# A gated attention and MLP kernel: smaller and reordered first loads, and a new order of the products that build the first K projection

## Chip, cores and metric

The kernel runs on one core of one Trainium2 chip. The metric is the device time of one execution in microseconds; a kernel is told by the median of several runs.

## What is computed

The reference takes `x` (2048 rows of 512), and gives `g * a + (1 - g) * b` in float32:

```python
g = _sigmoid((x * gate_w).sum(-1, keepdims=True))
qkv = x @ wqkv                       # 32 heads of 16
pq, pk = per-head q @ w_phi, k @ w_phi
phi = concat(softmax(p), softmax(-p))      # for q and for k
kv, z = phi_k^T v, sum over rows of phi_k
o = (phi_q kv) / (phi_q z + 1e-6)
a = o @ wo
b = mish(x @ w1 + b1) @ w2                 # 512 -> 1376 -> 512
```

The per-head 16 x 16 matrices `w_phi` come right behind the projections, so the kernel folds them into the weights first: `wk_fused = wk @ blockdiag(w_phi)`, and the same for `wq`. This folding is called "fusing" below.

## The kernel before, in words

**Precision.** The large products use `float32r` operands, one TensorE pass each. Every operand is split into a high part (a copy rounded to `float32r`) and a low part (the rest), and a product is the sum of three: high x high, high x low and low x high. The small fusing products and the warming products use plain float32; each of those shows as two MATMUL records in the profile.

**Stages.** Stage A goes through `x` in 8 chunks of 256 rows (`NCH`), two half-chunks `t` of 128 rows each: K, V and Q projections (`proj`, 12 products of 128x512 each, four blocks `k` of the contraction times three parts), feature maps, and a running sum of phi_k^T v (`kvp`). Stage B goes through 4 blocks of 512 rows: the MLP (`up`, `down`), attention (`num`) and the output product (`wo`). Texts such as `FIRST` and `EVEN` (lines 39 to 86) are the order of the steps, written out by hand, and `keep_in_program_order` (`pin`) keeps each engine's instructions in the order of the code.

**The opening**, which the change touches, stands ahead of the text `FIRST`:

- Loads (lines 139 to 166). SyncE (SP) issues, in this order: block 0 of the transposed K weights (`skT`, tensor `wkT`, 256 KB a block), blocks 0 and 1 of the first chunk of `x` (`rawx[0]`, 256 KB), K block 1, `x` blocks 2 and 3, K blocks 2 and 3, two pieces of the V weights (512 KB each), four blocks of the Q weights (`wqT`), the next chunk of `x`. ScalarE's own queue issues one load at the start: the block diagonal `bd` of `w_phi` into `bds` (256 KB, 2 KB a partition).
- Warming (lines 169 to 177). `warm(n)` multiplies a tile of ones by itself `n` times into a scratch bank and nothing reads it. `WARM` (line 34) is 10; two more stand behind the first fuse (line 706).
- Fusing K (lines 218 to 224 and 700 to 711). `fuse(acc, skT, k)` makes 16 float32 products of 64x64 out of K block `k` and `bds` into two PSUM banks; there are four such banks (tag `dn`), so two blocks are under way at a time. `fsplit(acc, k)` then makes the high part `wkh` of the block with two ScalarE copies, and the low part `wkl` with two VectorE subtractions.
- Splitting `x`. `x_hi(0, j)` is a ScalarE copy of `x` blocks `2j` and `2j+1` (128x512), and `x_lo(0, j, V)` a VectorE subtraction of the same shape.
- The first K projection. `k_part(k)` (line 692) makes the six products of block `k`: parts high x high, low(x) x high, high x low(w), each for the two half-chunks, into the two banks `pk`.

The loop of lines 700 to 714 says the order: fuse 0, two warming products, fuse 1; then x split 0, fsplit 0, x split 1, fsplit 1; then `k_part(0)`, `k_part(1)`; then fuse 2, fuse 3, fsplit 2 and fsplit 3. The split of the V weights follows on ScalarE, VectorE and GpSimd (lines 715 to 718), and then `k_part(2)` and `k_part(3)`. `FIRST` goes on with `fq` (the four fuses of the Q weights, line 724), and `v0`, the first V projection.

A helper records most operations under one line: all products have L101, ScalarE copies L121. They are told apart by the names of their tiles.

Of the kernel before, what the change touches and what calls it, by code (L numbers as in the profile page):

```python
# [15 lines left out]
P = 128  # L16
# [4 lines left out]
KT = D // P  # L21
NG = 4
SC = 256
# [7 lines left out]
NF = NFA + NFB  # L31
GROW = FA % P
ORDER = [NFA - 1] + list(range(NFA - 1)) + list(range(NFA, NF))
WARM = 10

# [52 lines left out]
def tile_gated_mix(ctx: ExitStack, tc: tile.TileContext, xT, wv, wkT, wqT, bd, w1a, w1b, b1, w2a, w2b, wo, out):  # L90
# [6 lines left out]
    pin = tc.keep_in_program_order  # L97
    V, G_, A_, Sy = nc.vector, nc.gpsimd, nc.scalar, nc.sync

    def mm(*a, **k):  # L100
        return pin(nc.tensor.matmul(*a, **k))  # L101
# [5 lines left out]
    def k8(name, tag, dt=F32R):  # L107
        return T([P, 2048], dt, tag, 2 if tag in ("eT", "E") else 1, name)

    def k4(name, tag, dt=F32):  # L110
        return T([P, 1024], dt, tag, {"tx": 2, "oh": 2, "z": 1}[tag], name)

    def k2(name, tag, dt=F32):
        return T([P, 512], dt, tag, {"pq": 3, "io": 4, "hl": 8}[tag], name)

    def psum(name, tag, bufs={"a": 3, "dn": 4, "kv": 1}):
        nm[0] += 1
        return pp.tile([P, 512], F32, name=f"{name}_{nm[0]}", tag=tag, bufs=bufs[tag])

    def act(out_, in_, fn=AF.Copy, **k):  # L120
        return pin(A_.activation(out_, in_, fn, **k))  # L121

    def kt(t, f):
        return t[:, : KT * f].rearrange("p (k f) -> p k f", f=f)
# [4 lines left out]
    def f32(ap):  # L129
        return ap.bitcast(F32)  # L130
# [5 lines left out]
    def stage(wT):  # L136
        return T([P, NFA * 512], F32, "w1a", 2, "wT")[:, : KT * 512].rearrange("p (k g f) -> p k g f", k=KT, f=P)

    skT, sqT = stage(wkT), stage(wqT)
    bds = k2("bds", "io")[:, :].rearrange("p (g f) -> p g f", g=NG)  # L140
    pin(A_.dma_start(bds, bd))
    rawx = {}

    def ldx(c):
# [3 lines left out]
    def ldk(dst, src, k):  # L148
        pin(Sy.dma_start(dst[:, k, :, :], src[:, k, :, :]))

    ldk(skT, wkT, 0)
    rawx[0] = k4("xraw", "tx")
    for j in range(2):
        pin(Sy.dma_start(kt(rawx[0], SC)[:, 2 * j : 2 * j + 2, :], xT[0][:, 2 * j : 2 * j + 2, :]))
        ldk(skT, wkT, j + 1)
    ldk(skT, wkT, 3)

    def piece(dram, o, n=1024):
        r = k4("raw", "oh")
# [13 lines left out]
    def warm(n):  # L173
        for _ in range(n):
            mm(pw[:, :P], ones, ones, start=True, stop=True)

    warm(WARM)
    onr = const.tile([P, P], F32R, name="onr")
# [25 lines left out]
    def run(text, key, prev=None, nxt=None):  # L204
# [6 lines left out]
    wkh, wkl, wvh, wvl, wqh, wql = [  # L211
        kt(k8(n, t), 512) for n, t in (("wkh", "xbh"), ("wkl", "xbl"), ("wvh", "woh"), ("wvl", "wol"), ("wqh", "eT"), ("wql", "eT"))]
    xs, Es, vs, psA, Ep = {}, {}, {}, {}, {}
# [4 lines left out]
    def fuse(acc, staged, k):  # L218

        for G in range(NG):  # L220
            o = (k % 2 * NG + G) * 64
            for r in (0, 64):
                for c in (0, 64):
                    mm(acc[r // 64][c : c + 64, o : o + 64], staged[r : r + 64, k, G, c : c + 64], bds[r : r + 64, G, r : r + 64], start=True, stop=True, skip_group_check=True)

    def fuse_banks():
        return [psum("fuse", "dn") for _ in range(2)]

    def halves(w, ks):
        return [w[:, ks, :].rearrange("p k (g r f) -> p r (k g) f", r=2, f=64)[:, r, :, :] for r in range(2)]  # L230
# [15 lines left out]
    def x_hi(c, j):  # L246
        act(xs[c][0][j], kt(rawx[c], SC)[:, 2 * j : 2 * j + 2, :])

    def x_lo(c, j, eng):
        pin(eng.tensor_sub(xs[c][1][j], kt(rawx[c], SC)[:, 2 * j : 2 * j + 2, :], f32(xs[c][0][j])))  # L250
# [430 lines left out]
    def fsplit(acc, k):  # L681
        wh, wl = halves(wkh, slice(k, k + 1)), halves(wkl, slice(k, k + 1))
        src = [a[:, k % 2 * 256 : k % 2 * 256 + 256].rearrange("p (g f) -> p g f", f=64) for a in acc]
        for r in range(2):
            act(wh[r], src[r])
        for r in range(2):
            pin(V.tensor_sub(wl[r], src[r], f32(wh[r])))

    new_x(0)
    pk = {}  # L690

    def k_part(k):
        for n, (a, w) in enumerate(((xs[0][0], wkh), (xs[0][1], wkh), (xs[0][0], wkl))):
            for t in range(2):
                sl = slice(t * P, (t + 1) * P)
                if t not in pk:
                    pk[t] = psum("proj", "a")
                mm(pk[t], a[k // 2][:, k % 2, sl], w[:, k, :], start=(k == 0 and n == 0), stop=(k == KT - 1 and n == 2))

    for ks in ((0, 1), (2, 3)):  # L700
        acc = []
        for k in ks:
            acc.append(fuse_banks())
            fuse(acc[-1], skT, k)
            if k == 0:
                warm(2)
        for k in ks:
            if k < 2:
                x_hi(0, k)
                x_lo(0, k, V)  # L710
            fsplit(acc[k % 2], k)
        if ks[0] == 0:
            k_part(0)
            k_part(1)
    for j in range(2):
        h, l = [w[:, 2 * j : 2 * j + 2, :].rearrange("p k f -> p (k f)") for w in (wvh, wvl)]
        act(h, wvr[j])
        pin((V, G_)[j].tensor_sub(l, wvr[j], f32(h)))
    k_part(2)
    k_part(3)  # L720

    accq = []

# [86 lines left out]
```

## Time and profile before

| what | value |
|---|---|
| median of 3 runs | 450.23 us (449.79, 450.23, 450.31) |
| the profiled execution | 449.95 us |
| its span, first to last instruction | 448.2 us |
| TensorE busy (PE) | 443.4 us, 99% of the span |
| VectorE, ScalarE, GpSimd busy | 307.0, 195.1, 164.7 us |
| chain that ended last | PE 98%, DMA 1% |
| Start of the first fuse, of the first K product | 5.95 us, 7.84 us |
| Start of the first fuse of the Q weights | 15.24 us |

Times inside the profile are microseconds from the start of the span. PE is a matrix product, PEld its weight load, DVE is VectorE, ACT ScalarE, POOL GpSimd, and SPq and ACTq are the issue of DMAs on SyncE's and ScalarE's queue. A row of the timeline gives start, duration, engine, line, operation, output <- inputs, shape, and how often it stands in a row; in brackets the idle time of the engine ahead of it and what ended that. Durations of neighbouring products overlap, so what a product costs is read from the distance of starts.

### The profile page before, as it was taken

The page shows a single profiled execution, that of the slowest core. Times are in us where ns is not written, and L with a number is a line of the kernel's source. Part 1 is how long each engine was busy: PE and PEld are TensorE (multiplying, and loading weights), DVE is VectorE, ACT ScalarE, POOL GpSimd, SP SyncE. Part 2 cuts the span into 40 slices and gives each one's busy share as a digit, 9 for nine tenths or more (in the row PEclk, how much of TensorE's full clock was granted, in tenths as well). Part 3 has the DMA queues.
Part 4 walks back from the last instruction along what each step waited for, and adds up shares of the span by engine and source line. Part 5 has one row for each costly group of instructions (what it writes and reads, how often), then busy time and mean ns, then how long its engine had stood idle before and what let it go on. Part 6 is the DMA issues. An engine that isn't in the chain of part 4 may idle for free.

```text
span 448.2 us, 7221 instructions
## 1 busy us (share of the span) xinstructions
PE 443.4 (99%) x2886; PEld 363.7 (81%) x2886; DVE 307.0 (68%) x408; ACT 195.1 (44%) x269; POOL 164.7 (37%) x102
## 2 busy tenths in 40 slices
PE   8999999999999999999999999999999999999997
PEld 7888888888888888878788878888878888887885
DVE  2798559459398999997989998369769329701103
ACT  3644533444335465627255352644262653242330
POOL 3448687677861445521122220214220222221121
PEclk9999999999999999999999999999999999999999
DMA  7721623615523100405243151321241302030002
GB/s 278 264 95 47 190 66 99 191 14 173 189 75 115 48 24 20 123 15 142 81 108 127 38 153 53 89 95 47 54 134 48 94 1 95 17 78 1 1 0 95
DMA packets 25882, 40.09 MB, mean 89 GB/s; under 512 B 5748, under 2 KB 14196, under 8 KB 25848
## 3 DMA queue, kind: packets, MB, share of 16 engines
q1 hardware_dynamic: 25528, 39.22, 29.2%
q8 instruction: 23, 0.38, 0.3%
q10 hardware_dynamic: 288, 0.39, 0.3%
q14 instruction: 11, 0.09, 0.1%
q0 software_dynamic: 32, 0.01, 0.0%
HBM read 22.82 MB, written 8.40 MB: 70 GB/s over the span
## 4 chain that ended last, share of the span: by engine, by line
PE 98%; DMA 1%; ACT 0%; DVE 0%; issue 0%
PE proj L101 30%; PE up L101 27%; PE down L101 27%; PE wo L101 10%; PE kvp L101 2%; PE num L101 2%; DMA bds<-in_bd_dram 1%; PE fuse L101 1%; PE rest L101 0%; PE z L101 0%; ACT wkh L121 0%; PE warm L101 0%; DVE io L653 0%; PE kvT L459 0%
## 5 line engine op out<-in xcount | busy, mean ns | idle before, releaser
L503 POOL TENSOR_TENSOR l<-act,h 128x512 fp32r<-128x512 f32 x44 | 63.8, 1452 | 218.1 <-ACT h L121 183.8
L121 ACT ACTIVATE act<-up,b1s 128x512 f32<-128x512 f32 x44 | 30.3, 689 | 92.1 <-PE up L101 91.2
L323 POOL TENSOR_TENSOR zacc<-zacc,E 128x1024 f32<-128x1024 f32 x16 | 39.8, 2485 | 43.9 <-DVE E L285 42.6
L121 ACT ACTIVATE E<-E 128x1024 f32<-128x1024 f32 x32 | 33.4, 1058 | 37.7 <-DVE E L270 37.6
L285 DVE TENSOR_TENSOR E<-E,Sm 128x1024 f32<-128x1024 f32 x32 | 46.6, 1456 | 1.1
L274 DVE TENSOR_REDUCE Sm<-E 128x64 f32<-128x1024 f32 x32 | 38.5, 1204 | 5.0 <-ACT E L121 5.0
L101 PE MATMUL wo<-woh,ohl 128*128 128x512 f32 x128 | 41.2, 389 | 0.0
L101 PE MATMUL down<-w2ah,h 128*128 128x512 f32 x96 | 37.7, 393 | 0.0
L101 PE MATMUL down<-w2al,h 128*128 128x512 f32 x96 | 37.4, 390 | 0.0
L101 PE MATMUL down<-w2ah,l 128*128 128x512 f32 x96 | 37.4, 389 | 0.0
L258 DVE TENSOR_REDUCE mx<-proj 128x32 f32<-128x512 f32 x16 | 11.0, 689 | 32.0 <-PE proj L101 32.0
L101 PE MATMUL down<-w2bh,h 128*128 128x512 f32 x78 | 30.6, 392 | 0.0
L101 PE MATMUL down<-w2bl,h 128*128 128x512 f32 x78 | 30.4, 390 | 0.0
L101 PE MATMUL down<-w2bh,l 128*128 128x512 f32 x78 | 30.3, 389 | 0.0
L408 DVE TENSOR_TENSOR xbl<-xraw,xbh 128x1024 fp32r<-128x1024 f32 x8 | 11.9, 1527 | 26.0 <-ACT xbh L121 26.0
L121 ACT ACTIVATE h<-act 128x512 fp32r<-128x512 f32 x44 | 27.8, 632 | 1.4
L101 PEld LDWEIGHTS wo<-woh,ohl 128*128 128x128 f32 x128 | 24.0, 188 | 5.0
L121 ACT ACT_TABLE_LOAD x19 | 24.4, 1283 | 5.5 <-PE up L101 5.2
L121 ACT ACTIVATE io<-wo,g_sb 128x512 f32<-128x512 f32 x16 | 10.9, 689 | 35.2 <-PE wo L101 35.2
L101 PE MATMUL up<-xbh,w1ah 128*128 128x512 f32 x96 | 25.8, 390 | 0.0
L101 PE MATMUL up<-xbl,w1ah 128*128 128x512 f32 x96 | 25.7, 389 | 0.0
L101 PE MATMUL up<-xbh,w1al 128*128 128x512 f32 x96 | 25.7, 389 | 0.0
(121 smaller groups left out, 968.4 us busy)
## 6 DMA issues: line engine op xcount, KB each, us to landing
eT<-E SPq DMA_DIRECT2D x128, 64.0 KB, 2.0
xraw<-in_xT_dram SPq DMA_DIRECT2D x15, 512.0 KB, 4.5
pqd<-qs SPq DMA_DIRECT2D x16, 256.0 KB, 3.1
pq<-pqd SPq DMA_DIRECT2D x16, 256.0 KB, 3.0
out_dram<-io SPq DMA_DIRECT2D x15, 256.0 KB, 2.4
raw<-in_w1a_dram SPq DMA_DIRECT2D x3, 512.0 KB, 4.1
raw<-in_w2a_dram SPq DMA_DIRECT2D x3, 512.0 KB, 4.2
wT<-in_wkT_dram SPq DMA_DIRECT2D x4, 256.0 KB, 5.2
```

The lines of the kernel that those rows point to most:

```text
L101: return pin(nc.tensor.matmul(*a, **k))
L121: return pin(A_.activation(out_, in_, fn, **k))
L258: pin(V.tensor_reduce(d[name], hv(src()), axis=AX.X, op=op))
L274: pin(V.tensor_reduce(d["S"], hv(d["E"][:, :]), axis=AX.X, op=ALU.add))
L285: pin(eng.tensor_mul(hv(d["E"][:, :]), hv(d["E"][:, :]), d["S"][:, :, None].to_broadcast([P, 2 * H, DH])))
L323: at(key, f"z{t}", lambda d=d: pin(G_.tensor_add(zacc, zacc, d["E"])))
L408: pin(V.tensor_sub(xb[b][1][:, :, sl], kt(raw[h], SC), f32(xb[b][0][:, :, sl])))
L503: pin(G_.tensor_sub(U[i]["l"], U[i]["a"], f32(U[i]["h"])))
```

## The change

Four edits, all in the opening:

- `WARM` is 9, and the two warming products behind the first fuse are gone.
- `bd` is loaded in two halves (128 KB each, 1 KB a partition): the first by SyncE ahead of all its other loads, the second by ScalarE's queue. The first half of `x` is loaded block by block: SyncE's order becomes half of `bd`, K 0, `x` 0, K 1, `x` 1, `x` 2 and 3, K 2, K 3.
- Fuses 0 and 1 stand together. `x` blocks 0 and 1 are split by VectorE alone and one block at a time (`x_one`: a copy 128x256 and a subtraction 128x256); ScalarE's first work is the fused parts. `x` blocks 2 and 3 are split as before, behind fsplit 1.
- `k_part` takes the part `n` as well: the order of the products is block 0 high x high, block 0 low x high, block 1 high x high, block 1 low x high, block 0 high x low; then fuses 2 and 3; then block 1 high x low, and blocks 2 and 3. Each entry is two products.

```diff
-WARM = 10
+WARM = 9
...
-    pin(A_.dma_start(bds, bd))
+    for eng, gs in ((Sy, slice(0, 2)), (A_, slice(2, 4))):
+        pin(eng.dma_start(bds[:, gs, :], bd[:, gs, :]))
...
-    for j in range(2):
-        pin(Sy.dma_start(kt(rawx[0], SC)[:, 2 * j : 2 * j + 2, :], xT[0][:, 2 * j : 2 * j + 2, :]))
-        ldk(skT, wkT, j + 1)
-    ldk(skT, wkT, 3)
+    for ks in (slice(0, 1), 1, slice(1, 2), slice(2, 4), 2, 3):
+        if isinstance(ks, int):
+            ldk(skT, wkT, ks)
+        else:
+            pin(Sy.dma_start(kt(rawx[0], SC)[:, ks, :], xT[0][:, ks, :]))
...
+    def k_part(k, n):
+        a, w = ((xs[0][0], wkh), (xs[0][1], wkh), (xs[0][0], wkl))[n]
+        for t in range(2):
...
+    def x_one(k):
+        r, h, l = kt(rawx[0], SC)[:, k, :], xs[0][0][0][:, k, :], xs[0][1][0][:, k, :]
+        pin(V.tensor_copy(h, r))
+        pin(V.tensor_sub(l, r, f32(h)))
+    def fused(ks):
+        acc = [fuse_banks() for _ in ks]
+        for a, k in zip(acc, ks):
+            fuse(a, skT, k)
+        return acc
...
+    acc = fused((0, 1))
+    x_one(0)
+    x_one(1)
+    fsplit(acc[0], 0)
+    fsplit(acc[1], 1)
+    x_hi(0, 1)
+    x_lo(0, 1, V)
+    for k, n in ((0, 0), (0, 1), (1, 0), (1, 1), (0, 2)):
+        k_part(k, n)
+    acc = fused((2, 3))
+    k_part(1, 2)
+    for k in (2, 3):
+        fsplit(acc[k - 2], k)
     for j in range(2):
         h, l = [w[:, 2 * j : 2 * j + 2, :].rearrange("p k f -> p (k f)") for w in (wvh, wvl)]
         act(h, wvr[j])
         pin((V, G_)[j].tensor_sub(l, wvr[j], f32(h)))
-    k_part(2)
-    k_part(3)
+    for k in (2, 3):
+        for n in range(3):
+            k_part(k, n)
```

More of the change, by code (lines that the diff above doesn't have):

```diff
@@ L690, in tile_gated_mix @@
     pk = {}
[L692 to L714, printed above, removed]
+    def k_part(k, n):
+        a, w = ((xs[0][0], wkh), (xs[0][1], wkh), (xs[0][0], wkl))[n]
+        for t in range(2):
+            sl = slice(t * P, (t + 1) * P)
+            if t not in pk:
+                pk[t] = psum("proj", "a")
+            mm(pk[t], a[k // 2][:, k % 2, sl], w[:, k, :], start=(k == 0 and n == 0), stop=(k == KT - 1 and n == 2))
+    def x_one(k):
[20 more added lines that the diff above has]
+        fsplit(acc[k - 2], k)
     for j in range(2):
```

## The prediction

> **What bounds the kernel now.** First the shares on the page, then the chain of work that ended last, in order of time.
>
> ```profile
> PE 443.4 (99%) x2886; PEld 363.7 (81%) x2886; DVE 307.0 (68%) x408; ACT 195.1 (44%) x269; POOL 164.7 (37%) x102
> PEclk9999999999999999999999999999999999999999
> PE 98%; DMA 1%; ACT 0%; DVE 0%; issue 0%
> 0.80 5.10 DMA bds<-in_bd_dram
> 11.56 0.67 ACT wkh L121 x2
> 17.33 27.43 PE proj L101 x120
> ```
>
> TensorE is the chain. It waits for something else only in the opening: for `bds` until 5.90, and once for `wkh`. From 17.33 on it runs product behind product, 27.43/120 = 0.229 us each. So what the opening gains or loses moves the end by as much, as long as everything behind it stays fed. The waits of TensorE over the whole span agree:
>
> ```profile
> PE warm L101 <- DVE ones L170: 1.1, 1, 1.1
> PE proj L101 <- ACT wkh L121: 0.3, 1, 0.3
> PE fuse L101 <- DMA bds<-in_bd_dram: 0.2, 1, 0.2
> ```
>
> Nothing after the opening makes it wait. The timeline of TensorE in the opening:
>
> ```profile
> 1.12 4.63 PE L101 MATMUL warm<-ones 128*128 128x128 f32 x20 [1.12 <-DVE ones L170]
> 5.95 0.69 PE L101 MATMUL fuse<-bds,wT 64*64 64x64 f32 x32 [0.19 <-DMA bds<-in_bd_dram]
> 6.57 0.71 PE L101 MATMUL warm<-ones 128*128 128x128 f32 x4
> 7.21 0.69 PE L101 MATMUL fuse<-bds,wT 64*64 64x64 f32 x32
> 7.84 0.73 PE L101 MATMUL proj<-wkh,xh 128*128 128x512 f32 x2
> 8.41 0.62 PE L101 MATMUL proj<-wkh,xl 128*128 128x512 f32 x2
> 10.83 1.16 PE L101 MATMUL fuse<-bds,wT 64*64 64x64 f32 x64
> 12.27 0.73 PE L101 MATMUL proj<-wkh,xh 128*128 128x512 f32 x2 [0.28 <-ACT wkh L121]
> 15.24 2.10 PE L101 MATMUL fuse<-bds,wT 64*64 64x64 f32 x128
> 17.26 1.19 PE L101 MATMUL proj<-wvh,xh 128*128 128x512 f32 x4
> ```
>
> Costs from the starts: a fuse ahead of other products 7.84 - 7.21 = 0.63; the four Q fuses 17.26 - 15.24 = 2.02, so each that follows another (2.02 - 0.63)/3 = 0.46, and a pair 1.09. Two products behind a fuse take 8.41 - 7.84 = 0.57, later pairs 2 x 0.229 = 0.46. Twelve take 10.83 - 7.84 = 2.99, or 15.24 - 12.27 = 2.97. Between fuses 2, 3 and the next product lie 12.27 - 10.83 = 1.44, so 0.35 of it is waiting for `wkh`.
>
> **Part one, the loads.** When the data land, from the views of the DMAs in narrow windows:
>
> ```profile
> 0.81 0.39 SPq L149 DMA_DIRECT2D wT<-in_wkT_dram  x1
> 1.71 0.43 SPq L149 DMA_DIRECT2D wT<-in_wkT_dram  x1
> bds<-in_bd_dram ACTq DMA_DIRECT2D x1, 256.0 KB, 5.1
> wT<-in_wkT_dram SPq DMA_DIRECT2D x1, 256.0 KB, 4.9
> wT<-in_wkT_dram SPq DMA_DIRECT2D x1, 256.0 KB, 5.4
> 6.49 0.63 ACT L121 ACTIVATE xh<-xraw 128x512 fp32r<-128x512 f32 x1 [3.65 <-DMA xraw<-in_xT_dram]
> 4.50:7.50 3.00, 2.81 (x59) 2.33 (x62) 0.35 (x1) 1.01 (x3) 0.00 (x0) 1.00 1.05 399
> ```
>
> K block 0 lands at 0.81 + 4.9 = 5.7, `bds` at 0.80 + 5.1 = 5.9, `x` 0 and 1 by 6.49, K block 1 at 1.71 + 5.4 = 7.11. Fuse 1 started at 7.21, 0.10 behind that: the two warming products fill a wait for K block 1 and cost little by themselves. At 399 GB/s (last number of the last row) a 128 KB block is 131/399 = 0.33 us. Fuse 0 needs the same 512 KB as before, so I put it at 5.85, an estimate: `bds` no longer lags behind K block 0, and nothing else is ahead. K block 1 has 128 KB of `x` less in front of it: 7.21 - 0.33 = 6.88 for fuse 1. `x` block 0 comes at 6.49 - 0.33 = 6.16, block 1 at about 7.2.
>
> The bounds. Early: fuse 1 follows fuse 0 at once, 5.85 + 0.46 = 6.31. Late: nothing is gained, 7.21; or later still, if packets are counted and not bytes. The halves of `bd` and the single `x` blocks have 1 KB a partition, so 640 packets stand up to the end of K block 1 instead of 512, and 128 packets more at the rate of 2 KB ones are 262/399 = 0.66 us, 7.54 (6.88 + 0.66). Rows for the packets, a store of 1 KB pieces in the last 8.3 us and the `bds` load in 0.8 to 5.4:
>
> ```profile
> q10 hardware_dynamic: 144, 0.13, 4.7%
> q10 hardware_dynamic: 143, 0.26, 17.6%
> ```
>
> 4.7% of 16 engines times 8.3 us is 6.2 us over 144 packets, 0.043 each; the 2 KB ones took 0.176 x 16 x 4.6/143 = 0.091. Half the size, half the time: I go by bytes, 6.88.
>
> The Trainium skill, "DMA: Bandwidth & Descriptors", section "Issuing engines are not separate DMA queues", says that DMAs issued from several engines run on the same 16 DMA engines and save issue time alone; by it the second queue gives nothing here, since one issue is 0.39, and the sum keeps only the gain of order. The trace agrees as far as it goes: 399 GB/s while SP's queue is alone at the end of that window.
>
> SP issues one load more. Loads also wait for older ones:
>
> ```profile
> SPq L160 <- DMA bds<-in_bd_dram: 1.6, 1, 1.6
> 3.84 2.41 SPq L160 DMA_DIRECT2D raw<-in_wv_dram  x2
> raw<-in_wv_dram SPq DMA_DIRECT2D x1, 512.0 KB, 6.7
> wT<-in_wqT_dram SPq DMA_DIRECT2D x1, 256.0 KB, 7.4
> ```
>
> The ninth load waits until the first landed. Now K block 3 is the ninth, so SP, and the V pieces and Q blocks behind it, stand until the first half of `bd` is there, before 5.9. V piece 1 used to leave at that time too, and the 256 KB blocks ahead are still moving, so I charge nothing. Without that cover K block 3 would come late for fuse 3, which starts at 10.5 below, four us on. The last Q block (issued at 8.02) lands at 15.4 and is needed at 15.9: a margin of 0.5. It caps the gain near 1.2.
>
> **Part two, the engines.** VectorE copies are not in the trace. Its nearest rows, with ScalarE's:
>
> ```profile
> L121 ACT ACTIVATE wkh<-fuse x8: 366/378/403, 7.0 to 12.4; 128x256 fp32r<-128x256 f32 x8
> L687 DVE TENSOR_TENSOR wkl<-fuse,wkh x8: 411/413/424, 7.8 to 13.0; 128x256 fp32r<-128x256 f32 x8
> L250 DVE TENSOR_TENSOR xl<-xraw,xh x2: 691/692/692, 7.2 to 8.7; 128x512 fp32r<-128x512 f32 x2
> 7.03 0.64 ACT L121 ACTIVATE wkh<-fuse 128x256 fp32r<-128x256 f32 x2
> 0.90 0.17 DVE L170 MEMSET ones<- 128x128 f32 x1 [0.90 <-PEq L800]
> ```
>
> A 128x256 copy lies between 0.17 (a smaller fill) and 0.69; I take 0.41, the same shape. VectorE: copy and subtraction of block 0 from 6.16 to 6.98; of block 1 from 7.2 to 8.0; `wkl` 0 until 8.85, `wkl` 1 until 9.65, low `x` 2, 3 until 10.35. ScalarE: `wkh` 0 behind fuse 0 (5.85 + 0.69) until 7.2, `wkh` 1 behind fuse 1 until 6.88 + 0.69 + 0.64 = 8.2. TensorE: fuse 1 at 6.88, products from 7.51; block 0 low x at 8.1 (ready 6.98); block 1 at 8.5 (8.2); its low x at 9.0 (8.0); block 0 low w at 9.45 (8.85); fuses 2 and 3 at 10.0 and 10.5, whose banks are free at 8.85 and 9.65; block 1 low w at 11.1 covers `wkh` 2 (10.0 + 0.69 + 0.64 = 11.35), needed at 11.7. Every margin is 0.3 or more, with copies at 0.69 too (`wkl` 0 at 9.4). If block 1 of `x` came 0.6 later than that, `wkl` 0 would be what is late.
>
> **The sum.** Fuse 1 at 6.88; + 0.63; ten products 2.97 - 0.46 = 2.51; pair of fuses 1.09; fourteen products 2.97 + 0.46 = 3.43. That is 14.54 for the first Q fuse against 15.24: 0.70 less. Where it comes from: 0.33 by the loads, 0.35 by the wait for `wkh`, 0.02 rounding; the removed products stood in a wait. Behind it, the V weights' low half:
>
> ```profile
> 14.74 2.46 POOL L718 TENSOR_TENSOR wvl<-raw,wvh 128x1024 fp32r<-128x1024 f32 x1 [10.42 <-ACT wvh L121]
> ```
>
> It ends at 17.2 even if nothing moves; it is first read seven products into V, 16.56 + 1.5 = 18.1. So the 0.70 reaches the end, and the profiled execution's 449.95 becomes 449.25.
>
> The median shown, 450.23, is 0.28 above that execution. One thing in the opening need not be alike in all of them:
>
> ```profile
> L101 PEld LDWEIGHTS warm<-ones x24: 186/333/333, 1.1 to 6.9; 128*128 128x128 f32 x24
> L101 PE MATMUL warm<-ones x24: 275/421/580, 1.1 to 7.0; 128*128 128x128 f32 x24
> ```
>
> The first products ran slower than the last four: weight loads 333 against 186 ns, 1.79 times (the row of the granted clock shows 9 throughout and doesn't tell). The rate rose between 5.95 and 6.57. If it rises later, fuse 0, the two warming products and fuse 1 all run slow: at (4.63 - 0.42)/19 = 0.22 apart the four records take 0.88, and no longer fit the wait. That costs before, and the changed kernel hasn't got it. I take 0.35 of the 0.88 (its part over 0.5 of cover) as saved in the median: 450.23 - 0.70 - 0.35 = **449.2**; without it 449.5.
>
> **Rivals.** *The loads bring nothing*: fuse 1 stays at 7.21, and only the wait for `wkh` goes: 450.23 - 0.35 = 449.9; if packets count, fuse 1 at 7.54, 450.2, with a copy or a late `x` block on top 450.5. For it: early packets are slow, 0.091 against 0.043 for half. Against: bytes fit the landings (0.7 apart). *The loads bring more*: fuse 1 right behind fuse 0, 1.27 less, and with the 0.35, 448.6. For it: `bds` landed last. Against: K block 1 is the fourth load still.
>
> *Slower*: the rate rises later. The first nine products end 0.43 earlier, leaving a gap of 0.5 until 5.85, and another of 0.5 ahead of fuse 1 with nothing in it. Before, TensorE worked for 4.9 us (1.12 to about 6) when the rate rose. If the gaps make it start over at 5.85, 4.9 us of work run at 1/1.79 of the rate: 4.9 x (1 - 1/1.79) = 2.2 late, and 449.2 + 2.2 = 451.4. It decides where fuse 0 falls ahead of the rise with too little work counted. Against it: 9 of 10 products are left and cover 1.12 to 5.3.
>
> The Trainium skill, "TensorE: Matmul & The Clock Gate", Part 1, says that the clock is released after about 3.4 us of sustained work, in a window that runs freely and not from the kernel's start. By it the nine products suffice, and the moment differs between executions; one such window later would cost about 3.4 x 0.44 = 1.5, an estimate from that page.
>
> **How the numbers follow.** Forecast 0.50 (448.9 to 449.6), loads bring nothing 0.20, more 0.12, slower 0.18. About 0.2% or 0.9 us, 449.33, is what a measurement here can tell from no change. Of the forecast's own 0.50 I put 0.38 under that line: faster 0.38 + 0.12 = 0.50, same 0.12 + 0.20 = 0.32, slower 0.18. The range leaves out the slower case: 448.6 to 450.5. The forecast by itself has 448.9 to 449.6.
>
> **What the profile would show.** Right: fuse 1 at 6.9 and products from 7.5; no wait for `wkh` at fuse 3; the first Q fuse near 14.5; warming loads at 333 ns and products from 7.5 on 0.23 apart. Wrong: fuse 1 at 7.2 or later (loads), a wait of TensorE on VectorE's `wkl` or on `wT` at the Q fuses, or K products 0.4 apart past 7 us (rate).

## The result and the profile after

The changed kernel takes 452.27 us (median of 6, 451.72 to 453.14) against 450.27 (6, 449.66 to 450.55): ratio 1.0048, interval 1.0038 to 1.0058. The ratio is of the means. It is 2.0 us slower; 1.0 less was forecast. The profiled execution took 452.56 with a span of 450.6.

The chain that ended last, in order of time, its opening:

```profile
2.20 5.99 DMA wT<-in_wkT_dram
8.19 0.04 issue
8.23 0.77 PE fuse L101 x32
9.01 3.97 PE proj L101 x10
12.98 1.09 PE fuse L101 x64
14.07 3.43 PE proj L101 x14
17.50 2.02 PE fuse L101 x128
19.52 27.43 PE proj L101 x120
```

Two rows carry the loss. The load of K block 1, issued at 2.20, lands at 8.19; before, issued at 1.71, it landed at 7.11. So 0.49 of the 1.08 us are its issue, since it is now the fourth load of SyncE's queue and not the third, and 0.59 its way from issue to landing (5.99 against 5.40). And ten products take 3.97, where 2.51 was worked out. The pair of fuses, 1.09, and the fourteen products, 3.43, are as forecast. From 19.52 on the chain is the 27.43 of before, begun 2.19 later (17.33), and TensorE's work behind the opening gains or loses nothing. The spans differ by 2.4 and these two executions by 2.61; the 0.4 that are left stand behind the last product or outside the span.

TensorE's timeline shows where it stood:

```profile
1.12 4.21 PE L101 MATMUL warm<-ones 128*128 128x128 f32 x18 [1.12 <-DVE ones L172]
5.26 0.69 PE L101 MATMUL fuse<-bds,wT 64*64 64x64 f32 x32
8.23 0.77 PE L101 MATMUL fuse<-bds,wT 64*64 64x64 f32 x32 [2.27 <-DMA wT<-in_wkT_dram]
8.94 1.22 PE L101 MATMUL proj<-wkh,xh 128*128 128x512 f32 x2
9.95 1.05 PE L101 MATMUL proj<-wkh,xl 128*128 128x512 f32 x2
10.81 1.05 PE L101 MATMUL proj<-wkh,xh 128*128 128x512 f32 x2
12.35 0.63 PE L101 MATMUL proj<-wkl,xh 128*128 128x512 f32 x2
12.91 1.16 PE L101 MATMUL fuse<-bds,wT 64*64 64x64 f32 x64
17.43 2.10 PE L101 MATMUL fuse<-bds,wT 64*64 64x64 f32 x128
```

Fuse 0 starts at 5.26, 0.7 sooner than before: its data really come earlier. Then TensorE stands for 2.27 us, and the first products behind are 0.43 apart ((10.81 - 9.95)/2) and not 0.23. The windows view, whose last three columns are the granted clock, the share of time in which the DMA engines were busy (a little over 1 is possible) and GB/s, says why:

```profile
2.00:4.00 2.00, 2.00 (x11) 2.00 (x11) 0.00 (x0) 0.84 (x2) 1.98 (x5) 1.00 0.86 240
4.00:6.00 2.00, 1.96 (x39) 1.60 (x37) 0.72 (x2) 0.00 (x1) 0.32 (x1) 1.00 0.93 198
6.00:8.00 2.00, 0.00 (x0) 0.00 (x0) 0.00 (x0) 0.65 (x2) 0.00 (x0) 1.00 0.83 249
8.00:10.00 2.00, 1.77 (x35) 1.46 (x36) 1.42 (x5) 0.98 (x3) 0.00 (x0) 0.68 1.03 388
10.00:12.00 2.00, 2.00 (x6) 1.61 (x5) 1.23 (x3) 0.20 (x1) 0.00 (x0) 0.50 1.03 418
12.00:14.00 2.00, 2.00 (x69) 1.43 (x67) 0.00 (x0) 0.36 (x2) 0.00 (x0) 0.97 1.06 397
```

Read two columns. GB/s: the loads crawl at 198 to 249 from 4 to 8 us. Before, the slow stretch lay at 2 to 4 us, with 157 GB/s, and 399 followed from 4.5 on. Up to 8 us the changed kernel has read (240 + 198 + 249) x 2 = 1374 KB; the kernel before, at 157, 370 and 405 GB/s in the same windows, 1864 KB:

```profile
2.00:4.00 2.00, 2.00 (x11) 2.00 (x11) 0.00 (x0) 0.83 (x2) 1.98 (x5) 1.00 0.69 157
```

Clock: 0.32 x 2 + 0.50 x 2 + 0.03 x 2 = 1.7 us are lost to a granted clock of 0.5, which makes a stretch of 3.4 us that begins about 0.5 us behind the standstill. Five of the six executions have a mean clock of 0.994 to 0.996, which has room for such a loss (1.7 us are 0.004 of 450). The sixth, 453.14, has 0.999, which has not; where it lost its time, no trace shows.

### The profile page after: what moved, and what is told of

It reads as the page before. It is cut to its first block, busy times and chain, and to the rows that moved or that the text cites. A ratio compares the mean times of both kernels' runs of the same rounds, so it can differ in the third digit from the quotient of the medians.

```text
span 450.6 us, 7213 instructions
## 1 busy us (share of the span) xinstructions
PE 443.7 (98%) x2880; PEld 363.9 (81%) x2880; DVE 307.7 (68%) x411; ACT 194.6 (43%) x268; POOL 164.8 (37%) x102
## 4 chain that ended last, share of the span: by engine, by line
PE 97%; DMA 1%; SPq 0%; DVE 0%; issue 0%
PE proj L101 30%; PE up L101 27%; PE down L101 26%; PE wo L101 10%; PE kvp L101 2%; PE num L101 2%; DMA wT<-in_wkT_dram 1%; PE fuse L101 1%; PE rest L101 0%; PE z L101 0%; DVE io L655 0%; PE kvT L461 0%; SPq L158 0%; SPq L150 0%; SPq L142 0%
```

## The experiments

Theory **L**: the four changed loads make K block 1 late, and the gap brings the slow clock. Rival **W**: the missing warming products bring the slow clock, whatever the loads do. Each ratio is of the means, against the kernel before on the same chip, with its interval; a row stands for 3 (run 10) to 12 executions (run 1), and each profile shows one of them.

| run | what differs | median (lowest to highest), us | ratio |
|---|---|---|---|
| 1 | changed, loads of before | 449.69 (449.36 to 451.99) | 1.0006 (0.9994 to 1.0018) |
| 2 | before, changed loads | 452.05 (451.58 to 453.39) | 1.0048 (1.0036 to 1.006) |
| 3 | changed, nine products in the gap | 450.98 (450.3 to 451.49) | 1.002 (1.0011 to 1.0029) |
| 4 | before, fewer warming products | 450.39 (450.0 to 451.69) | 1.0013 (1.0005 to 1.0022) |
| 5 | changed, `bd` whole on ScalarE's queue | 450.19 (449.67 to 450.36) | 1.0004 (0.9994 to 1.0013) |
| 6 | changed, `x` in pairs | 453.56 (451.53 to 454.19) | 1.0074 (1.0053 to 1.0094) |
| 7 | loads of before, all warming products | 449.62 (449.39 to 450.13) | 0.9995 (0.9986 to 1.0003) |
| 8 | both halves on ScalarE's queue | 451.12 (450.05 to 452.74) | 1.0022 (1.0008 to 1.0036) |
| 9 | `bd` whole, first on SyncE's queue | 451.64 (450.59 to 451.97) | 1.0032 (1.002 to 1.0045) |
| 10 | `bd` in halves by partitions | 451.94 (451.69 to 453.18) | 1.005 (1.0032 to 1.0067) |
| 11 | as 5, `WARM` 10 | 449.68 (449.04 to 450.11) | 0.9991 (0.9982 to 1.0) |
| 12 | as 11, two products in the gap | 449.77 (449.15 to 450.34) | 0.9996 (0.9987 to 1.0005) |
| 13 | `bd` whole, second on SyncE's queue | 450.96 (450.06 to 451.91) | 1.0025 (1.0015 to 1.0036) |
| 14 | changed, GpSimd's small load later | 451.14 (450.65 to 452.99) | 1.0032 (1.0018 to 1.0047) |

### Loads or warming products: runs 1 to 4

Run 1 puts the loads back:

```diff
-    for eng, gs in ((Sy, slice(0, 2)), (A_, slice(2, 4))):
-        pin(eng.dma_start(bds[:, gs, :], bd[:, gs, :]))
+    pin(A_.dma_start(bds, bd))
...
-    for ks in (slice(0, 1), 1, slice(1, 2), slice(2, 4), 2, 3):
-        if isinstance(ks, int):
...
+    for j in range(2):
+        pin(Sy.dma_start(kt(rawx[0], SC)[:, 2 * j : 2 * j + 2, :], xT[0][:, 2 * j : 2 * j + 2, :]))
+        ldk(skT, wkT, j + 1)
+    ldk(skT, wkT, 3)
```

> The changed kernel with the loads of before: bd whole on ScalarE's queue, x in two pairs of blocks; all else as changed. Theory L (the new sizes and order of the loads make K block 1 land at 8.2 instead of 7.1, and the gap of 2.3 us that this leaves brings the slow rate): fuse 1 back at 7.2, K products 0.23 apart, first Q fuse near 14.9, time about 450.27 - 0.35 = 449.9. Theory W (the warming products that are gone let the rate fall, whatever the loads do): a stretch of 3.4 us with a granted clock of 0.5 remains, 450.27 + 1.2 = 451.5 or more.

The median, 449.69, is near L's 449.9, but five of twelve executions took 450.95 to 451.99, and the means show no gain. The profiled one is one of the five (450.95). Its timeline:

```profile
5.75 2.34 PE L101 MATMUL fuse<-bds,wT 64*64 64x64 f32 x64 [0.41 <-DMA bds<-in_bd_dram]
8.01 1.22 PE L101 MATMUL proj<-wkh,xh 128*128 128x512 f32 x2
9.88 1.01 PE L101 MATMUL proj<-wkh,xh 128*128 128x512 f32 x2
8.00:10.00 2.00, 2.00 (x9) 1.60 (x6) 1.76 (x5) 1.18 (x3) 0.00 (x0) 1.00 1.04 425
```

No wait for K block 1 here, but the pair of fuses takes 2.26 and four products 9.88 - 8.01 = 1.87, 0.47 apart: the rate had not risen yet by 9.9. The granted clock of the last row is 1.00 all the same, so that column doesn't show a rise that comes late, and the distance of starts has to tell. So W has a part of its own, in some executions.

Run 2 is the kernel before with the two load edits of the change alone.

> The kernel before with the four changed loads alone (bd in halves on two queues, x by blocks); ten and two warming products and the old order of engines stay. Theory L: fuse 1 at 8.2 with a wait of TensorE on K block 1 of 1.5 us in spite of the two warming products, time 451.3 (wait alone) to 452.3 (with the slow rate). Theory W: the loads are harmless, 450.0 to 450.3.

452.05: the loads alone make the whole loss, with all twelve warming products in place. Its profile, of a slower execution (453.24), has K block 1 late, then a wait for `wkh`, since ScalarE's copy of `x` waits for the late block 1 of `x`, and the clock at 0.5 behind the two waits:

```profile
7.76 0.69 PE L101 MATMUL fuse<-bds,wT 64*64 64x64 f32 x32 [0.57 <-DMA wT<-in_wkT_dram]
9.43 1.17 PE L101 MATMUL proj<-wkh,xh 128*128 128x512 f32 x2 [0.97 <-ACT wkh L121]
10.00:12.00 2.00, 2.00 (x6) 1.62 (x5) 1.49 (x4) 0.53 (x2) 0.00 (x0) 0.50 1.03 413
```

Only two of its six executions (453.24 and 453.39) have the mean clock of 0.996 that goes with this stretch. The other four, 451.58 to 452.05, have 0.999 or 1.0. Their loss is the loads' too, but how it divides into waiting and a late rise of the rate isn't shown.

Run 3 keeps the late load and fills the gap:

```diff
             fuse(a, skT, k)
+            if k == 0:
+                warm(9)
```

> The changed kernel with nine warming products between fuse 0 and fuse 1, where TensorE stood still for 2.3 us (two records each, 0.11 apart at the fast rate: 2.0 us; 3.9 us if they run slow). If the slow stretch comes from the gap: granted clock 1.0 throughout behind the first rise, products 0.23 apart, first Q fuse at 8.23 + 7.66 = 15.9 instead of 17.4, time 452.27 - 1.5 = 450.8. If the slow stretch has another cause, 452.3 as it is; if the products themselves run slow they push fuse 1 to 9.6 and the time to 453 or more.

```profile
5.92 2.27 PE L101 MATMUL warm<-ones 128*128 128x128 f32 x18
8.13 0.69 PE L101 MATMUL fuse<-bds,wT 64*64 64x64 f32 x32
15.74 2.09 PE L101 MATMUL fuse<-bds,wT 64*64 64x64 f32 x128
```

From fuse 1 to the first Q fuse it is 7.61, against 9.20 in the changed kernel and 7.66 in the forecast. By the ratios, 1.0048 and 1.002, filling the gap saves 0.0028 x 450 = 1.3 us: that is what the slow clock behind the gap costs in the mean of the executions. The late block with all else in the change costs 0.002 x 450 = 0.9.

Run 4 is the kernel before with `WARM = 9` and without `warm(2)`.

> The kernel before with nine warming products at the start and none behind fuse 0; loads and order as before. Theory L: fuse 1 waits for K block 1 until 7.2 as before, gaps of 0.4 and 0.6 us only, rate stays up, 450.2 to 450.3 (no change). Theory W: the rate falls or rises late, 451.3 or more.

450.39, ratio 1.0013: small and clear of no change; six of eleven executions took 450.0 to 450.4, five 450.8 to 451.7. No trace of the five was kept, and two of them (451.22 and 451.69) have spans of 448.4 and 449.0, 2.7 to 2.8 us less than their times where 1.7 to 1.9 is usual in the kernel before, so part of their loss lies outside the span. W, which run 1's profile shows, is not what made the 2 us.

### Which load: runs 5, 6, 8, 9, 10, 13, 14

Run 5 has `pin(A_.dma_start(bds, bd))` in the changed kernel, run 6 the old pairs of `x` blocks.

> The changed kernel with bd loaded whole by ScalarE's queue as before; x stays in the new order (block 0, K 1, block 1, blocks 2 and 3). Theory H (the halves of bd, one of them ahead of all on SyncE's queue, bring the first loads early and put the slow stretch of the loads, 160 to 250 GB/s, behind them, on K block 1): slow stretch back at 2 to 4.5 us, K block 1 lands near 6.8, time 449.7 to 451.5 with two groups of executions as in the kernel with all old loads. Theory X (the single x blocks with 1 KB a partition, read between the K blocks, slow the reading): K block 1 near 8, time 452.

> The changed kernel with x in two pairs of blocks as before; bd stays in halves on two queues. Theory H: the slow stretch stays behind 4 us, K block 1 lands at 7.7 or later, time 452. Theory X: K block 1 near 6.8, time 449.7 to 451.5. If both this and the run with whole bd are fast, it takes the two together; if both are slow, each does it.

Theory H holds, X falls. Run 5, with the single `x` blocks:

```profile
5.54 1.77 PE L101 MATMUL fuse<-bds,wT 64*64 64x64 f32 x64 [0.21 <-DMA bds<-in_bd_dram]
14.45 2.28 PE L101 MATMUL fuse<-bds,wT 64*64 64x64 f32 x128
```

K block 1 is there when fuse 0 ends, and the first Q fuse starts at 14.45 where 14.54 was forecast. Run 6, with the halves, has four executions, and the profiled one (454.19) is its slowest:

```profile
8.54 0.69 PE L101 MATMUL fuse<-bds,wT 64*64 64x64 f32 x32 [2.16 <-DMA wT<-in_wkT_dram]
4.00:6.00 2.00, 2.00 (x35) 1.78 (x37) 0.00 (x0) 0.00 (x0) 0.33 (x1) 1.00 0.70 179
6.00:8.00 2.00, 0.38 (x16) 0.21 (x8) 0.50 (x2) 0.66 (x2) 0.00 (x0) 1.00 0.95 253
```

What of the halves does it? Runs 8, 9 and 10 change the line of `bd` alone:

```diff
+    for eng, gs in ((A_, slice(0, 2)), (A_, slice(2, 4))):        # run 8, 1 KB a partition
+    pin(Sy.dma_start(bds, bd))                                    # run 9, 2 KB, first on SyncE
+    for eng, ps in ((Sy, slice(0, 64)), (A_, slice(64, 128))):    # run 10, 2 KB, by partitions
```

> The changed kernel with both halves of bd (1 KB a partition each) issued by ScalarE's queue, none by SyncE. Theory P (the size of the pieces: 1 KB pieces pass quickly, all early loads are early and the slow stretch falls on K block 1): K block 1 lands near 8, time 452. Theory Q (the place on SyncE's queue: a half ahead of K block 0 shifts what is read while): K block 1 lands near 6.5, time 450.2 as with the whole bd.

> The changed kernel with bd whole (2 KB a partition) as SyncE's first load and nothing on ScalarE's queue. Theory P: K block 1 lands near 6.5 to 7, since the pieces are large, time 450.2. Theory Q: bd ahead of K block 0 on SyncE's queue makes K block 1 land near 8, time 452.

> The changed kernel with bd in halves by partitions (64 partitions each, 2 KB pieces) on the same two queues. Theory P: K block 1 near 6.5, time 450.2. Theory Q: K block 1 near 8, time 452, like the halves of the change.

Fuse 1 in the three, in this order:

```profile
6.82 0.69 PE L101 MATMUL fuse<-bds,wT 64*64 64x64 f32 x32 [0.19 <-DMA wT<-in_wkT_dram]
```

```profile
8.02 0.69 PE L101 MATMUL fuse<-bds,wT 64*64 64x64 f32 x32 [1.63 <-DMA wT<-in_wkT_dram]
```

```profile
7.54 0.69 PE L101 MATMUL fuse<-bds,wT 64*64 64x64 f32 x32 [0.98 <-DMA wT<-in_wkT_dram]
```

P, the size of the pieces, falls: 1 KB pieces on ScalarE's queue leave K block 1 in time (run 8), 2 KB ones ahead of K block 0 on SyncE's make it late (run 9). Q holds as to K block 1 in these two. Run 10 decides less than it seems: in its profile SyncE's first issues took longer, and K block 1 was issued only at 2.85, landing 4.7 us later, which is less than the 5.4 of before:

```profile
2.85 0.43 SPq L150 DMA_DIRECT2D wT<-in_wkT_dram  x1
```

Run 8's time missed Q's 450.2. In its profiled execution, the slowest of five (452.74), the Q weights come late, with the loads at 242 GB/s in 8 to 10 us:

```profile
16.54 2.04 PE L101 MATMUL fuse<-bds,wT 64*64 64x64 f32 x96 [1.08 <-DMA wT<-in_wqT_dram]
8.00:10.00 2.00, 2.00 (x13) 1.37 (x12) 1.84 (x5) 0.72 (x2) 0.00 (x0) 1.00 0.76 242
```

Run 13 moves `pin(Sy.dma_start(bds, bd))` of run 9 behind K block 0; run 14 is the changed kernel with GpSimd's load of `b1` behind the text `FIRST`.

> The changed kernel with bd whole on SyncE's queue as its second load, behind K block 0 instead of ahead of it; nothing on ScalarE's queue. If the place ahead of K block 0 is what matters: K block 1 lands near 6.5 to 7, 449.7 to 450.3. If it matters that ScalarE's queue has no 256 KB load beside SyncE's: K block 1 near 8, 451.2 to 452, as with bd whole and first.

> The changed kernel with GpSimd's own small load (b1, 5.5 KB in pieces of 44 bytes), which runs at 5.0 to 7.9 in the changed kernel, moved behind the first chunk. If that load is what stalls the others: no slow stretch behind 4.5, K block 1 lands by 6, first Q fuse near 14, 449.2. If it only shares the slow stretch: K block 1 near 8, 452.

```profile
2.18 0.43 SPq L148 DMA_DIRECT2D wT<-in_wkT_dram  x1
6.70 0.69 PE L101 MATMUL fuse<-bds,wT 64*64 64x64 f32 x32 [0.62 <-DMA wT<-in_wkT_dram]
10.75 1.38 PE L101 MATMUL fuse<-bds,wT 64*64 64x64 f32 x64 [0.83 <-DMA wT<-in_wkT_dram]
6.00:8.00 2.00, 1.38 (x42) 1.14 (x36) 1.28 (x4) 1.23 (x4) 0.00 (x0) 1.00 0.96 269
```

Run 13 is neither case: K block 1 is in time, but a slow stretch follows (269 GB/s) and K block 2 is late, 450.96. An obvious rival is the later issue: every load of `bd` on SyncE's queue ahead of K block 1 makes that block the queue's fourth, issued near 2.2 and not at 1.71. Run 13 has this too (2.18, first row), and its fuse 1 starts at 6.70. So the later issue alone doesn't make K block 1 late; the place of `bd` ahead of K block 0 does. That `bd` on SyncE's queue still costs in run 13 can come from the later issues or from the missing load on ScalarE's queue; the runs don't tell these apart. In run 14 fuse 1 waits for K block 1 until 7.70, the loads move at 181 and 220 GB/s from 4 to 8 us, and the time is 451.14: GpSimd's load is not what makes them slow. Its ratio, 1.0032, is below the changed kernel's 1.0048, and the intervals overlap; whether the small load costs something of its own was not told apart.

**Open.** That loads run slow somewhere in the first 10 us is in every profile; that `bd` on SyncE's queue ahead of K block 0 brings a slow stretch onto K block 1 is shown by runs 2, 6, 9 and 14 (fuse 1 at 7.70 to 8.54) against 5, 8 and 13 (6.82 or sooner), in one profiled execution each. Why the DMA engines read slowly there, and why the order of the first loads shifts and lengthens it, is not settled.

### Putting the good parts together: runs 7, 11, 12

Run 7 is run 1 with `WARM = 10` and `warm(2)` between fuses 0 and 1; run 11 is run 5 with `WARM = 10`; run 12 is run 11 with that `warm(2)`.

> The changed kernel with the loads of before, ten warming products at the start and two between fuse 0 and fuse 1: what is left of the change is the order of fuses, copies and K products. Theory L with the rate as a second step: no slow stretch behind 7 us in any execution, so one group of executions near 449.5 (0.5 less than before, by the wait for wkh of 0.35 and little more). Theory W alone (number of warming products decides): the same. If the new order of engines itself invites the slow rate: again two groups, 449.5 and 451.

> The changed kernel with bd whole on ScalarE's queue as before and ten warming products at the start; x by blocks and the order of engines stay as changed. Fuse 0 at 5.55 to 5.6, fuse 1 at once, first Q fuse near 14.5; if the tenth product keeps the rate from rising late, one group of executions at 449.5 to 449.7 and not a second one at 450.3: 0.5 less than before.

> The changed kernel with bd whole on ScalarE's queue, ten warming products at the start and two between fuse 0 and fuse 1; x by blocks and the order of engines as changed. If what held the former two candidates back (449.6 and 449.7) is a late K block 1 with TensorE idle and then the rate, the two products cover it: 449.4 to 449.6 and a spread of executions under 0.6. If K block 1 lands by 6.5 in most executions, the two products cost their 0.44 and it is 449.8 or more.

449.62, 449.68 and 449.77, ratios 0.9995, 0.9991 and 0.9996: at best 0.4 us (0.0009 of 450), with an interval that just touches no change. Run 7's profiled execution, 449.49, has its first Q fuse at 14.68, 0.56 ahead of before, and is 0.46 shorter than before's; over all executions its gain is 0.2, and not clear of none. Its spread, 449.39 to 450.13, against run 1's to 451.99 shows what the three missing warming products are for. Run 11 still waited for K block 1 in its profiled execution, and run 12's filler didn't make the time better. Run 11:

```profile
6.92 0.69 PE L101 MATMUL fuse<-bds,wT 64*64 64x64 f32 x32 [0.95 <-DMA wT<-in_wkT_dram]
14.55 2.47 PE L101 MATMUL fuse<-bds,wT 64*64 64x64 f32 x128
16.96 1.20 PE L101 MATMUL proj<-wvh,xh 128*128 128x512 f32 x4
```

The first Q fuse at 14.55 is 0.69 ahead of before, but the four Q fuses then take 2.41 and not 2.02, so part of the gain is given back there. The last two Q blocks took 8.1 us from issue to landing, against 7.5 and 7.4 before, which would explain it; the waits view names no releaser for this idle time, so it stays an inference.

## Why the prediction was wrong

**The step that failed** is in part one: "K block 1 has 128 KB of `x` less in front of it: 7.21 - 0.33 = 6.88 for fuse 1." It was 8.23, and outside the bounds 6.31 and 7.54 too. The upper bound was added up wrongly: if packets are counted, the 0.66 goes on top of 7.21, since 6.88 has already taken off bytes, and that is 7.87; 8.23 lies outside this as well. The step moved a landing along a rate of 399 GB/s, read from 4.5 to 7.5 of the old order, and put two things at nothing without a reason: the later issue of K block 1 (0.49 us), and that the slow 2 to 4 us (157 GB/s) could move. With `bd` ahead on SyncE's queue the loads were slow at 4 to 8 us (198 and 249 GB/s), on the very block whose landing was worked out; why they slow down there stays open. In the sum, first Q fuse at 14.54, it is this: fuse 1 came 1.35 later, took 0.14 longer, and the ten products behind it 1.46 longer. The last two are the slow clock, which the sum did not have. Together they are 2.95, and the first Q fuse stands at 17.50 in the chain. The same step also missed the other way: fuse 0, taken at 5.85, started at 5.26. What came early was the block that didn't decide.

The rule of the Trainium skill, "DMA: Bandwidth & Descriptors", section "Issuing engines are not separate DMA queues", that all queues share 16 DMA engines and a further issuer saves issue time alone, was said to agree. Runs 9 and 13 speak against reading it as "the queue doesn't matter": the same 256 KB on SyncE's queue cost 1.5 and 0.8 us more than on ScalarE's (451.64 and 450.96 against 450.19; ratios 1.0032 and 1.0025 against 1.0004), and the issue that ScalarE's queue saves is 0.47 (2.18 against 1.71 for K block 1).

**The rival "slower"** named the right engine state and a time 0.9 short of the measured one (451.4), by a wrong course, so its nearness is in part luck: it expected the rate to rise late. The rate rose in time and fell behind the gap. Its "another of 0.5 ahead of fuse 1 with nothing in it" became 2.27. It was priced at 2.2 and cost 1.3 (run 3). That the rate can also rise late with the old loads in place is borne out by run 1's profile.

The Trainium skill, "TensorE: Matmul & The Clock Gate", Part 1, has a window of 3.4 us that decides between half and full clock; the trace agrees on the length, with 1.7 us lost at 0.5, a stretch of 3.4. A standstill shorter than that, 2.27 us, was enough here to bring it.

**Steps that held.** Everything between fuse 1 and the first Q fuse: 7.66 worked out, 7.61 in run 3 and 14.68 - 7.06 = 7.62 in run 7:

```profile
7.06 0.69 PE L101 MATMUL fuse<-bds,wT 64*64 64x64 f32 x32
14.68 2.10 PE L101 MATMUL fuse<-bds,wT 64*64 64x64 f32 x128
```

No wait for `wkh` at fuses 2 and 3, so the 0.35 is gone. VectorE's copy was costed at 0.41 and took 0.29:

```profile
5.14 0.29 DVE L706 CAST xh<-xraw 128x256 fp32r<-128x256 f32 x1 [4.07 <-DMA xraw<-in_xT_dram]
```

**A size that was off**: the 0.35 us added for executions in which the rate rises late had the wrong sign. Fewer warming products cost the kernel before 0.6 us (450 x 0.0013) and opened the spread of run 1. It also rested on a misreading: the rate was said to rise between 5.95 and 6.57, but the 32 weight loads of fuse 0, from 5.95 on, took 129 to 135 ns, and 178 to 228 where that fuse ran slow (run 9). The rate had risen before fuse 0. With the parts that held, run 5 gives no change and run 7 0.2 us, not 1.0.

## What to carry to other kernels

When loads are reordered, don't carry a landing time along the old order's bandwidth: read the bandwidth by windows, ask what is being moved in the slow stretch, and what the new order puts there. Idle time of TensorE early in a kernel can cost twice, once as the wait and once as the slow clock behind it, so products that look idle may be what keeps the clock; a spread of executions that widens when they go is the sign.

## What the runs showed of the hardware that was not expected

- A standstill of 2.27 us, behind 4.8 us of work (1.12 to 5.96), was enough for 3.4 us at a granted clock of 0.5, and so were two of 0.57 and 0.97 in run 2. One of 1.63 (run 9) was not, in its one profiled execution, where the ten products behind fuse 1 ran at full rate (rows below). There fuse 0 had still run slow (1.13 and not 0.69), so the two cases differ in more than the gap, and three of run 9's five executions have a mean clock of 0.996. The length of the gap alone doesn't decide.
- The place of `bd` shifted the stretch of slow loads (157 GB/s at 2 to 4 us before) to 4 to 8 us (198 and 249 GB/s) and made it longer; the size of its pieces, 1 or 2 KB, did not decide that for K block 1 (runs 8 and 9).

```profile
5.26 1.13 PE L101 MATMUL fuse<-bds,wT 64*64 64x64 f32 x32
8.65 0.73 PE L101 MATMUL proj<-wkh,xh 128*128 128x512 f32 x2
11.15 1.16 PE L101 MATMUL fuse<-bds,wT 64*64 64x64 f32 x64
```

Ten products in 11.15 - 8.65 = 2.50.
